# An attention and two-MoE kernel: the first unit's weights P transposed by TensorE instead of by DMA, with work moved between VectorE and ScalarE

## The chip, the cores and the metric

The kernel runs on one core of one Trainium2 chip. The metric is the device time of one execution in microseconds (us). The profile is of one execution, taken by the hardware profiler; the engines in it are PE (TensorE matmul), PEld (TensorE weight load), DVE (VectorE), ACT (ScalarE), POOL (GpSimd) and SP (SyncE, which issues the DMAs here).

## The reference

Three stages, all in float32, on 4 batches of 576 tokens:

```python
scores = scale * q @ k.T                      # 8 heads of 64, causal
bias = -(cum[:, :, :, None] - cum[:, :, None, :])   # cum: running sum of max(s, 0)
attn = softmax(where(causal, -1e9, scores + minimum(bias, 0)))
x = attn @ v                                  # heads joined: (4, 576, 512)
# first MoE
xk = mu_k * x + (1 - mu_k) * x_prev;  xr = mu_r * x + (1 - mu_r) * x_prev
x = sigmoid(xr @ w_r) * (maximum(xk @ w_k, 0) ** 2 @ w_v)
# second MoE
h = maximum(x @ w_in, 0);  u, v = halves of h
v_n = (v - mean) / sqrt(var + 1e-6)
out = (u * (w_spatial @ v_n + b_spatial)) @ w_out
```

The weights arrive as float64 and are turned into float32 on the chip ("decoded", three integer operations of DVE for each block).

## The kernel before, in words

The tokens are cut into nine units of 256. For batch b, A*b* is the first 256 tokens, B*b* the next 256; the last 64 of every batch form the unit T. The order of the attention is ORDER (L48): A0, A1, B0, A2, B1, A3, B2, B3. The first MoE takes the units in the same order, with T before the last of them.

**Attention.** An `Item` (L334) is one head of one unit: kind "G0" is a head of an A unit (two tiles of 128 queries, 128 and 256 keys wide), "G1" a head of a B unit (384 and 512 keys), "T" the tail of a pair of heads (576 columns). `scores` puts the scores in PSUM (tag "s", three banks), `softmax` masks them and takes the row's extreme on DVE (L388) and exponentiates on ACT (L396), and `norm` makes the weights P = e * r, split in two float16 parts: the first part hi by ACT (L429) if the item's kind and batch stand in HI_ACT (L29), else by DVE (L431); the second part lo, the rest, always by DVE (L433). P (three buffers) is then transposed by a DMA issued from SP into eT (L435): for G0 six blocks of 128x128, 192 KB. `pv` (L453) multiplies eT with the parts of v on PE (L479) into one PSUM buffer, and `scaled` brings the result x to SBUF, by ACT (L486) if the kind stands in X_ACT (L31), else by DVE (L488). It comes two items after the pair's last one (PV_LAG). For A0, `first_mix` follows each pair at once: the difference d on POOL (L606, recorded at the helper's line L204), then two operations of DVE that make xm (L608). Four pairs of heads, p = 0 to 3, give the four contraction blocks k = 0 to 3 of the first MoE's matmul.

**First MoE.** For each unit eighteen groups in the order of `seq` (L850): A (L624, `w_k`, eight groups), C (L656, `w_v`, eight, into the PSUM tile cps of tag "c", one buffer) and B (L640, `w_r`, two). ACT evacuates A with a Relu and a Square (L630, L632) from two PSUM buffers.

**Weights.** `w_k` is cut into eight blocks, `w_v` into eight and `w_r` into four; the last two are a list of twelve jobs (L846). A job issues a 512 KB load into one of three buffers (tag "b4"), and `load_double` decodes it on DVE (L509, L512, L514). `weights(n)` (L702) decodes n blocks and keeps three loads ahead. It is called with 8 after A0's attention (the blocks of `w_k`), with W_RATE = 3 before every MoE group (L866), and with 1 after every second attention step past A0 (L788, W_STEP = 2).

**Order.** The attention's steps are laid between the MoE's groups by `target` (L859), which spreads the steps of a unit over a range of groups given by MKS. What stands in the code is not the order on the queues: the program is built with a scheduler that orders each engine's instructions by simulated time (L1137), and each engine then runs its queue in that order.

**Second MoE** (from L881) comes last and is not touched.

Of the kernel before, what the change touches and what calls it, by code (L numbers as in the profile page):

```python
# [7 lines left out]
F32 = mybir.dt.float32  # L8
F32R = mybir.dt.float32r
F16 = mybir.dt.float16  # L10
BF16 = mybir.dt.bfloat16
I32 = mybir.dt.int32
AF = mybir.ActivationFunctionType
# [11 lines left out]
UN = 256  # L25
NU = NTOK // UN
PSC = 32768.0
PV_LAG = 2
HI_ACT = ("G00", "G01", "G10", "T0")  # L29
SQ = "PPPPPDAAD"  # L30
X_ACT = ("2",)  # L31
SQLO = "PPPPPDPPP"
V_STT = (0, 1, 2, 3)
MKS = (10, 9, 0, -2, 2, -2, -2, -2)
W_RATE = 3
W_STEP = 2
W_PRE = 5
W_0 = 2
W_1 = 0
# [8 lines left out]
ORDER = ("A0", "A1", "B0", "A2", "B1", "A3", "B2", "B3")  # L48
# [17 lines left out]
def kernel(  # L66
# [18 lines left out]
    nc = tc.nc  # L85

    def f32(ap):
# [14 lines left out]
    ap_ = at.enter_context(tc.tile_pool(name="att", bufs=1, side="right", reuse_waits="tile"))  # L102
    ps1 = ExitStack()
    pp = ps1.enter_context(tc.tile_pool(name="ps1", bufs=1, space=PSUM, reuse_waits="tile"))
# [10 lines left out]
        out=mask[:, 384:512], in_=mask[:, 384:512], pattern=[[-1, 128]], compare_op=ALU.is_ge,  # L115
        fill=-8.0e9, base=0, channel_multiplier=1)
    nc.gpsimd.memset(maskt, 0.0)
    for g in range(2):
        a = slice(64 * g, 64 * g + 64)
        nc.gpsimd.affine_select(  # L120
            out=maskt[a, 224:288], in_=maskt[a, 224:288], pattern=[[-1, 64]], compare_op=ALU.is_ge,
            fill=-8.0e9, base=0, channel_multiplier=1)

    ident = ap_.tile([128, 128], F32, name="ident")
    nc.gpsimd.memset(ident, 1.0)
    nc.gpsimd.affine_select(
        out=ident, in_=ident, pattern=[[-1, 128]], compare_op=ALU.is_equal, fill=0.0, base=0,
        channel_multiplier=1)

# [74 lines left out]
    def half(g):  # L206
        return slice(64 * g, 64 * g + 64)
# [109 lines left out]
        vparts[b, p] = ((hl[:, 0], hl[:, 1]), PROD3, vm[:, 1:2])  # L317

    eT = {}

    def get_eT(kind, b, p, h=None):
        key = (kind, b, p, h)
        if key not in eT:
            if kind == "1":
                eT[key] = ap_.tile([128, 2, 2, 3, 128], F16, tag="eT1", name="eT1", bufs=T1B)
            elif kind == "2":
                eT[key] = ap_.tile([128, 14, 128], F16, tag="eT2", name="eT2", bufs=T2B)
            else:
                t = ap_.tile([128, 2, 2, 3, 128], F16, tag="eT1", name="eTt", bufs=T1B)
                t = t.rearrange("p a l c i -> p (a l c) i")[:, 0:10]  # L330
                eT[key] = t.rearrange("p (l c) i -> p l c i", l=2)
        return eT[key]

    class Item:  # L334
# [66 lines left out]
        def norm(self):  # L401
            st, e = self.st, self.e
            n = 1 if self.kind == "T" else 2
            nc.vector.tensor_scalar(
                out=st[:, 4:4 + n], in0=st[:, 2:2 + n], scalar1=1e-9, scalar2=1.0 / PSC,
                op0=ALU.add, op1=ALU.mult)
            nc.vector.reciprocal(out=st[:, 6:6 + n], in_=st[:, 4:4 + n])
            P = ap_.tile([128, 1792], F16, tag="P", name="P", bufs=PB)
            if self.kind == "T":
                Pv = P[:, 0:1280].rearrange("p (l c) -> p l c", l=2)  # L410
                nc.gpsimd.memset(Pv[:, :, 576:640], 0.0)
                jobs = [(st[:, 6:7], e[:, 0:576], Pv[:, 0, 0:576], Pv[:, 1, 0:576])]
                dst, nb = get_eT("T", self.b, self.p).rearrange("p l c i -> p (l c) i"), 10
            elif self.kind == "G0":
                Pv = P[:, 0:768].rearrange("p (l c) -> p l c", l=2)
                jobs = [
                    (st[:, 6:7], e[:, 0:128], Pv[:, 0, 0:128], Pv[:, 1, 0:128]),
                    (st[:, 7:8], e[:, 128:384], Pv[:, 0, 128:384], Pv[:, 1, 128:384]),
                ]
                dst = get_eT("1", self.b, self.p)[:, self.h % 2].rearrange("p l c i -> p (l c) i")  # L420
                nb = 6
            else:
                jobs = [
                    (st[:, 6:7], e[:, 0:384], P[:, 0:384], P[:, 384:768]),
                    (st[:, 7:8], e[:, 384:896], P[:, 768:1280], P[:, 1280:1792])]
                dst, nb = get_eT("2", self.b, self.p, self.h), 14
            for r, ein, hi, lo in jobs:
                if self.kind + str(self.b) in HI_ACT:
                    nc.scalar.activation(out=hi, in_=ein, func=AF.Copy, scale=r)  # L429
                else:  # L430
                    nc.vector.tensor_scalar(out=hi, in0=ein, scalar1=r, scalar2=None, op0=ALU.mult)  # L431
            for r, ein, hi, lo in jobs:
                nc.vector.scalar_tensor_tensor(  # L433
                    out=lo, in0=ein, scalar=r, in1=hi, op0=ALU.mult, op1=ALU.subtract)
            nc.sync.dma_start_transpose(out=dst, in_=P[:, 0:128 * nb])  # L435

# [4 lines left out]
    def get_x(key):  # L443
        if key not in xT:
            if key == "T":
                xT[key] = mp.tile([128, NP, B, 65], F32, tag="xt", name="xt")
            else:
                xT[key] = mp.tile([128, NP, UN + 1], F32, tag="x", name="x", bufs=XB)
                if key[0] == "A":
                    nc.gpsimd.memset(xT[key][:, :, 0:1], 0.0)  # L450
        return xT[key]

    def pv(b, p, kind):  # L453
        vt, PROD, esc = vparts[b, p]
        ps = pp.tile([128, 256], F32, tag="pv", name="pvps")
        if kind == "T":
            e = get_eT("T", b, p)
            n = len(PROD)
            for c in range(5):
                for i, (a, l) in enumerate(PROD):  # L460
                    nc.tensor.matmul(  # L461
                        ps[:, 0:128], vt[a][:, c], e[:, l, c],
                        start=(c == 0 and i == 0), stop=(c == 4 and i == n - 1))
        else:
            nch = 2 if kind == "1" else 4
            for c in range(nch):
                for i, (a, l) in enumerate(PROD):
                    for g in range(2):
                        h = 2 * p + g
                        if kind == "1":  # L470
                            e = get_eT("1", b, p)[:, g, l]
                            mv = e[:, 0:2] if c == 0 else e[:, 2:3]
                            t0 = c
                        else:
                            e = get_eT("2", b, p, h)
                            t0 = max(c - 2, 0)
                            o = 3 * l + c
                            mv = e[:, o:o + 7 + l:6 + l] if c < 3 else e[:, 9 + 4 * l:10 + 4 * l]
                        nc.tensor.matmul(  # L479
                            ps[64 * g:64 * g + 64, 128 * t0:256], vt[a][:, c, 64 * g:64 * g + 64], mv,  # L480
                            start=(c == 0 and i == 0), stop=(c == nch - 1 and i == len(PROD) - 1))

        def scaled(out, in_, a=slice(0, 128)):
            by = 1.0 / PSC if esc is None else esc[a]
            if kind in X_ACT:
                nc.scalar.activation(out=out, in_=in_, func=AF.Copy, scale=by)  # L486
            else:
                nc.vector.tensor_scalar(out=out, in0=in_, scalar1=by, scalar2=None, op0=ALU.mult)  # L488

        def evac():  # L490
            done.add((b, p, kind))
            if kind == "T":
                x = get_x("T")
                for g in range(2):
                    a = half(g)
                    scaled(x[a, p, b, 1:65], ps[a, 64 * g:64 * g + 64], a)
            else:
                x = get_x(("A" if kind == "1" else "B") + str(b))
                scaled(x[:, p, 1:UN + 1], ps)
        return evac  # L500
# [55 lines left out]
    def row_blocks(kc, n):  # L556
        return [(slice(k, k + 1), slice(0, n)) for k in range(kc)]
# [144 lines left out]
    def weights(n, ahead=2):  # L702
        for _ in range(n):
            while wjobs and len(wq) <= ahead:
                wq.append(wjobs.pop(0)())
            if wq:
                wq.pop(0)()

    late = []
    ends = {}  # L710
# [71 lines left out]
    pos = [0]  # L782

    def att_to(n):
        while pos[0] < min(n, len(steps)):
            steps[pos[0]]()
            pos[0] += 1
            if pos[0] > ends[ORDER[0]] and pos[0] % W_STEP == 0:  # L788
                weights(1)

    fs = ExitStack()
    fp = fs.enter_context(tc.tile_pool(name="first", bufs=1, side="left", reuse_waits="tile"))
# [50 lines left out]
    wvp = m1.enter_context(tc.tile_pool(name="wv", bufs=1, side="left", reuse_waits="tile"))  # L843
    W["r"], jr = load_weights("wr", wp, w_r, 4, DM, tmp1, col_blocks(4, DM))
    W["v"], jv = load_weights("wv", wvp, w_v, 8, DM, tmp1, row_blocks(8, DM))
    wjobs += jv[0:4] + jr + jv[4:8]  # L846

    groups = []
    for u in range(NU):
# [15 lines left out]
    for gi, (u, kind, m) in enumerate(groups):  # L865
        weights(W_RATE)  # L866
        ev = {"A": moe_A, "B": moe_B, "C": moe_C}[kind](u, m)
# [75 lines left out]
    for i in range(2):  # L943
        a, o = half(i), half(1 - i)
# [197 lines left out]
```

## Time and profile before

| what | us |
|---|---|
| median of three runs | 734.26 (730.25 to 735.81) |
| the profiled execution | 729.34 |
| its span, first to last instruction | 727.6 |
| PE busy in the span | 675.8 (93%) |
| DVE busy | 476.8 (66%) |
| ACT busy | 345.2 (47%) |
| first matmul of the first MoE with the last pair's input (k = 3) begins | 60.49 |

How to read it: the span is what the rows below divide; the 1.7 us between the span and the execution lie around it and are not in any row. A busy share is a mean over stages with different limits, so the rows are taken stage by stage. A bracket such as [1.29 <-DMA eT<-P] gives the idle time of the engine ahead of the instruction and what released it.

### The profile page before, as it was taken

The numbers are of one execution on the slowest core, as the hardware profiler recorded it, in microseconds if no ns is written. First come the engines' busy times: TensorE is split into PE (matmuls) and PEld (weight loads), VectorE is DVE, ScalarE is ACT, GpSimd is POOL, SyncE is SP. The second block draws the span as 40 slices with busy tenths as digits, with TensorE's granted clock in tenths as the row PEclk, the third lists the DMA queues.
The fourth block names the chain that finished last, engine by engine and source line by source line (L and its number), as shares of the span: only waits on it lengthen the run. The fifth ranks groups of instructions, "written<-read, shape, count | busy, mean of one in ns | idle before, by whom it ended". The sixth has DMA issues, their size and how long they took to land.

```text
span 727.6 us, 11854 instructions
## 1 busy us (share of the span) xinstructions
PE 675.8 (93%) x4168; PEld 594.6 (82%) x4168; DVE 476.8 (66%) x1251; ACT 345.2 (47%) x860; POOL 170.7 (23%) x186
## 2 busy tenths in 40 slices
PE   4577999998988999989988999999989999999998
PEld 3455887886877888868877888888888998998998
DVE  7999488778798878998999394030776235035031
ACT  3345359644545676747654423142564343233222
POOL 6114033210432353534432144000540000000000
PEclk9997999999999999999999999999999999999999
DMA  8999368666749787778966731061610110100101
GB/s 231 264 246 222 99 140 185 144 125 139 171 101 179 160 176 190 172 148 202 199 143 124 168 115 59 0 193 50 192 36 16 66 33 1 66 2 1 66 1 66
DMA packets 137027, 88.93 MB, mean 122 GB/s; under 512 B 111396, under 2 KB 120804, under 8 KB 136968
## 3 DMA queue, kind: packets, MB, share of 16 engines
q1 hardware_dynamic: 136968, 88.17, 50.1%
q8 instruction: 33, 0.54, 0.3%
q14 instruction: 26, 0.21, 0.1%
HBM read 52.22 MB, written 9.68 MB: 85 GB/s over the span
## 4 chain that ended last, share of the span: by engine, by line
PE 44%; DVE 7%; issue 2%; DMA 1%; ACT 1%; POOL 0%; SPq 0%; ACTq 0%; DVEq 0%
PE dps L1029 8%; PE dps L1050 7%; PE mmps L624 6%; PE cps L656 6%; PE dps L1009 6%; PE dps L976 6%; PE mmps L640 2%; DVE xm L595 1%; DVE P L433 1%; DVE P L431 1%; DMA wsr<-in_w_spT_dram 1%; PE pvps L479 1%; DVE e L388 1%; PE pvps L461 1%; DVE b L512 1%
## 5 line engine op out<-in xcount | busy, mean ns | idle before, releaser
L624 PE MATMUL mmps<-xm,wk 128*128 128x256 f32 x576 | 143.8, 391 | 5.1 <-ACT e L396 3.0
L656 PE MATMUL cps<-sq,wv 128*128 128x256 f32 x576 | 138.7, 382 | 0.0
L624 PEld LDWEIGHTS mmps<-xm,wk 128*128 128x128 f32 x576 | 109.9, 195 | 22.6 <-ACT e L396 3.2
L656 PEld LDWEIGHTS cps<-sq,wv 128*128 128x128 f32 x576 | 109.1, 191 | 15.0
L396 ACT ACTIVATE e<-e,st 128x128 f32<-128x128 f32 (+3 forms) x128 | 70.8, 554 | 79.3 <-DVE st L388 78.8
L433 DVE SCALAR_TENSOR_TENSOR P<-e,st,P 128x512 f16<-128x512 f32 (+4 forms) x144 | 92.8, 666 | 3.9 <-ACT P L429 3.2
L204 POOL TENSOR_TENSOR kl<-raw,kh 64x576 fp32r<-64x576 f32 (+1 forms) x40 | 55.3, 1382 | 145.6 <-ACT kh L240 124.0
L640 PE MATMUL mmps<-xm,wr 128*128 128x256 f32 x288 | 66.5, 381 | 0.0
L640 PEld LDWEIGHTS mmps<-xm,wr 128*128 128x128 f32 x288 | 54.7, 191 | 7.5
L388 DVE CUSTOM_DVE_ANT_0 e<-sps,mask 128x128 f32<-128x128 f32 (+3 forms) x128 | 57.9, 482 | 1.9 <-PE sps L363 1.1
L630 ACT ACTIVATE kk<-mmps 128x256 f32<-128x256 f32 x72 | 26.8, 374 | 62.4 <-PE mmps L624 62.2
L431 DVE TENSOR_SCALAR P<-e,st 128x128 f16<-128x128 f32 (+3 forms) x92 | 43.4, 509 | 2.2 <-issue 0.4
L363 PE MATMUL sps<-raw 66*128 66x128 f32 (+1 forms) x96 | 28.4, 454 | 13.9 <-DMA raw<-c 10.5
L204 POOL TENSOR_TENSOR qh<-raw,qh 64x320 fp32r<-64x320 f32 (+1 forms) x40 | 40.6, 1015 | 0.2
L665 DVE SCALAR_TENSOR_TENSOR xo<-rg,cps 128x512 f32<-128x512 f32 x18 | 11.6, 679 | 42.6 <-PE cps L656 42.6
L1050 PE MATMUL dps<-gl,woh 128*128 128x288 f32 x128 | 38.2, 298 | 0.0
L1050 PE MATMUL dps<-gh,wol 128*128 128x288 f32 x128 | 38.1, 297 | 0.0
L1050 PE MATMUL dps<-gh,woh 128*128 128x288 f32 x128 | 37.8, 296 | 0.0
L1009 PE MATMUL dps<-x2h,wih 128*128 128x288 f32 x128 | 37.8, 295 | 0.0
L1009 PE MATMUL dps<-x2l,wih 128*128 128x288 f32 x128 | 37.8, 295 | 0.0
L1009 PE MATMUL dps<-x2h,wil 128*128 128x288 f32 x128 | 37.7, 295 | 0.0
L1029 PE MATMUL dps<-wsh,vnh 128*128 128x288 f32 x128 | 37.7, 295 | 0.0
(172 smaller groups left out, 1449.9 us busy)
## 6 DMA issues: line engine op xcount, KB each, us to landing
raw<-in_qkb_dram SPq DMA_DIRECT2D x32, 448.0 KB
vr<-in_v_dram SPq DMA_DIRECT2D x24, 320.0 KB
out_dram<-o SPq DMA_DIRECT2D x32, 144.0 KB
b<-in_w_v_dram SPq DMA_DIRECT2D x8, 512.0 KB
x_d<-xo SPq DMA_DIRECT2D x16, 256.0 KB
b<-in_w_in_dram SPq DMA_DIRECT2D x8, 512.0 KB
raw<-in_qka_dram SPq DMA_DIRECT2D x12, 256.0 KB
b<-x_d SPq DMA_DIRECT2D x8, 288.0 KB
```

The costliest lines, as they stand in the source:

```text
L204: nc.gpsimd.tensor_tensor(out=out, in0=in0, in1=in1, op=ALU.subtract)
L388: nc.vector.tensor_tensor_reduce(out=e[:, off:off + W], in0=self.ps[i], in1=mask[:, 512 - W:512], scale=-0.125, scalar=3.0e38, op0=ALU.add ...
L396: nc.scalar.activation(out=e[:, off:off + W], in_=e[:, off:off + W], func=AF.Exp, scale=-1.0, bias=st[:, i:i + 1], accum_out=st[:, 2 + i:3 ...
L431: nc.vector.tensor_scalar(out=hi, in0=ein, scalar1=r, scalar2=None, op0=ALU.mult)
L433: nc.vector.scalar_tensor_tensor(out=lo, in0=ein, scalar=r, in1=hi, op0=ALU.mult, op1=ALU.subtract)
L624: nc.tensor.matmul(ps[:, 0:UN], W["k"][:, k, 128 * m:128 * m + 128], mix[u, "k"][:, k], start=(k == 0), stop=(k == 3))
L640: nc.tensor.matmul(o, W["r"][:, k, 128 * m:128 * m + 128], mix[u, "r"][:, k], start=(k == 0), stop=(k == 3))
L656: nc.tensor.matmul(cps[u][:, m], W["v"][:, k, 128 * m:128 * m + 128], sq[u, k], start=(k == 0 and m % 2 == 0), stop=(k == 7 and m % 2 == 1))
L976: nc.tensor.matmul(ps, a[:, k, j:j + 128], w[:, k, 512:1024], start=(n == 0), stop=(n == 11))
L1009: nc.tensor.matmul(ps[:, 0:HB], w[:, k, 128 * m:128 * m + 128], a[:, k, HB * hf:HB * hf + HB], start=(n == 0), stop=(n == 11))
L1029: nc.tensor.matmul(ps[:, 0:HB], vn, ws, start=(n == 0), stop=(n == len(pairs) - 1))
L1050: nc.tensor.matmul(ps[:, 0:HB], w[:, k, 128 * m:128 * m + 128], a[:, k], start=(n == 0), stop=(n == 11))
```

## The change

The list of jobs changes in one line: five blocks of `w_v` stand ahead of those of `w_r` instead of four. The call of `weights` in `att_to` goes, and W_RATE falls from 3 to 1. HI_ACT gains the A units of batches 2 and 3 and the B unit of batch 1. X_ACT keeps all B units ("2") and gains the A units of batches 0 and 1 ("10", "11"). A0's eight items are transposed by six PE instructions each into a PSUM tile of tag "c" (the tag of cps), half a tile for each head of a pair, and one ACT copy brings each head's result to eT.

```diff
-HI_ACT = ("G00", "G01", "G10", "T0")
+HI_ACT = ("G00", "G01", "G02", "G03", "G10", "G11", "T0")
-X_ACT = ("2",)
+X_ACT = ("20", "21", "22", "23", "10", "11")
-W_RATE = 3
-W_STEP = 2
+W_RATE = 1
...
+    idh = ap_.tile([128, 128], F16, name="idh")
+    nc.gpsimd.tensor_copy(idh, ident)
...
+    turned = {}
...
-            nc.sync.dma_start_transpose(out=dst, in_=P[:, 0:128 * nb])
+            if self.kind == "G0" and self.b == 0:
+                self.transpose(P, dst, nb)
+            else:
+                nc.sync.dma_start_transpose(out=dst, in_=P[:, 0:128 * nb])
+
+        def transpose(self, P, dst, nb):
+            if self.h % 2 == 0:
+                turned[self.p] = pp.tile([128, 4, UN], F32, tag="c", name="tps")
+            ps = turned[self.p].bitcast(F16).rearrange("p (g a) n -> p g (a n)", g=2)[:, self.h % 2]
+            for i in range(nb):
+                j = slice(128 * i, 128 * i + 128)
+                nc.tensor.transpose(ps[:, j], P[:, j], idh)
+            nc.scalar.activation(
+                out=dst.rearrange("p l i -> p (l i)"), in_=ps[:, 0:128 * nb], func=AF.Copy)
...
-            if kind in X_ACT:
+            if kind + str(b) in X_ACT:
...
-            if pos[0] > ends[ORDER[0]] and pos[0] % W_STEP == 0:
-                weights(1)
...
-    wjobs += jv[0:4] + jr + jv[4:8]
+    wjobs += jv[0:5] + jr + jv[5:8]
```

## Rows read from the trace of the kernel before

**Rows 1.** Windows by stage: PE, PEld, DVE, ACT, POOL busy, clock, DMA share, GB/s.

```profile
20.00:42.00 22.00, 14.68 (x80) 10.87 (x82) 21.63 (x68) 8.40 (x30) 2.99 (x5) 1.00 0.94 248
42.00:48.00 6.00, 4.20 (x19) 3.44 (x16) 5.40 (x20) 2.77 (x10) 1.31 (x3) 1.00 1.04 226
48.00:60.50 12.50, 6.22 (x51) 4.15 (x50) 12.50 (x40) 6.79 (x22) 5.24 (x6) 0.83 0.97 254
60.50:67.00 6.50, 6.26 (x17) 4.06 (x19) 6.50 (x17) 5.07 (x16) 4.58 (x4) 0.53 0.75 205
67.00:107.00 40.00, 40.00 (x246) 34.35 (x243) 27.22 (x69) 18.08 (x43) 8.45 (x9) 1.00 0.62 139
107.00:450.00 343.00, 324.60 (x2045) 276.96 (x2044) 290.81 (x809) 197.54 (x503) 115.74 (x117) 0.99 0.69 154
450.00:727.60 277.60, 270.49 (x1695) 253.31 (x1693) 96.97 (x189) 99.12 (x216) 19.83 (x14) 0.99 0.17 52
```

**Rows 2.** Timeline of PE: start, us, line, operation, count, idle before and releaser.

```profile
23.24 0.37 PE L479 MATMUL pvps<-eT,vr 128*64 128x256 f16 x1 [1.29 <-DMA eT<-P]
...
48.77 1.36 PE L479 MATMUL pvps<-eT,vr 128*64 128x256 f16 x20
...
50.18 0.92 PE L363 MATMUL sps<-raw 66*128 66x128 f32 x4
...
60.49 2.07 PE L624 MATMUL mmps<-xm,wk 128*128 128x256 f32 x4 [0.48 <-DVE xm L608]
...
63.15 3.68 PE L624 MATMUL mmps<-xm,wk 128*128 128x256 f32 x8 [0.24 <-ACT kk L630]
...
67.48 1.99 PE L624 MATMUL mmps<-xm,wk 128*128 128x256 f32 x8
...
104.62 1.00 PE L461 MATMUL pvps<-eTt,vhl 128*128 128x128 f16 x15
```

**Rows 3.** Timeline of DVE in the first unit.

```profile
16.36 0.75 DVE L433 SCALAR_TENSOR_TENSOR P<-e,st,P 128x256 f16<-128x256 f32 x1
...
41.43 0.47 DVE L433 SCALAR_TENSOR_TENSOR P<-e,st,P 128x256 f16<-128x256 f32 x1
...
53.83 0.41 DVE L488 TENSOR_SCALAR x<-pvps 128x256 f32<-128x256 f32 x1
...
59.98 0.46 DVE L608 SCALAR_TENSOR_TENSOR xm<-d,muk,x 128x256 f32<-128x256 f32 x1
```

**Rows 4.** Timeline of POOL: the last pair's d, with what runs ahead.

```profile
55.70 1.31 POOL L204 TENSOR_TENSOR qh<-raw,qh 64x320 fp32r<-64x320 f32 x1
57.09 0.68 POOL L204 TENSOR_TENSOR d<-x 128x256 f32<-128x256 f32 x1
```

**Rows 5.** Windows of DVE's decoding alone: wv in the first two, wr in the third.

```profile
30.00:42.00 12.00, 3.93 (x7) 1.00 0.79 184
42.00:60.40 18.40, 3.13 (x5) 0.89 0.98 245
...
42.00:60.40 18.40, 5.93 (x9) 0.89 0.98 245
```

**Rows 6.** Groups of instructions by line: count, busy us, mean ns.

```profile
L431 DVE TENSOR_SCALAR P<-e,st 128x128 f16<-128x128 f32 (+3 forms) x92 | 43.4, 509 | 2.2 <-issue 0.4
L630 ACT ACTIVATE kk<-mmps 128x256 f32<-128x256 f32 x72 | 26.8, 374 | 62.4 <-PE mmps L624 62.2
L429 ACT ACTIVATE P<-e,st 128x128 f16<-128x128 f32 (+4 forms) x52 | 25.3, 534 | 10.5 <-DVE st L407 8.9 <-ACT e L396 1.5
L647 ACT ACTIVATE rg<-mmps 128x512 f32<-128x512 f32 x18 | 10.2, 585 | 16.3 <-PE mmps L640 16.3
```

**Rows 7.** Waits of PE: us in total, times, longest.

```profile
PE mmps L624 <- ACT e L396: 3.0, 1, 3.0
...
PE sps L349 <- ACT x L486: 2.4, 1, 2.4
```

## The prediction

> **What bounds the kernel now.** I read the windows by stage first [rows 1], because PE's 93% is a mean. From 67 to 107 us PE is busy for 40.00 of 40.00 us; from 107 to 450 it lacks 18.4 us (343.0 - 324.6); behind 450 it lacks 7.1 in a stage that the change leaves alone. The holes are in front: 7.3 us from 20 to 42, 1.8 from 42 to 48, 6.3 from 48 to 60.5, together 15.4. In the same stretches DVE is full: 21.63 of 22.0, 5.40 of 6.0, 12.50 of 12.5, 6.50 of 6.5. So up to 67 us the first unit, A0, is made by a saturated DVE while PE waits for it, and afterwards PE sets the pace, with DVE at 85% (290.8 of 343) close behind.
>
> Second I read the timelines of PE, DVE and POOL along A0's end. The last P of A0 is finished at 41.90 (41.43 + 0.47) [rows 3]. The products of the last pair begin at 48.77 and end at 50.13 [rows 2]. DVE takes the result x at 53.83, 3.7 us later [rows 3]; POOL forms d at 57.09, 2.9 us after x was there, straight behind the qh part of a split of heads for a later unit [rows 4]; DVE makes xm at 59.98, 2.2 us after d ended at 57.77 [rows 3]; PE begins the fourth contraction block at 60.49 [rows 2], and the first MoE can run. From the last P to that matmul 18.6 us pass, of which the work itself is about 4.
>
> Third, what stood in front of A0 on DVE: decoding of wv took 3.93 us between 30 and 42, and wv and wr together 9.06 (3.13 + 5.93) from 42 to 60.4 [rows 5]. That work is not needed before the first MoE runs.
>
> Fourth, PE's clock. [...] The twelve matmuls at 60.49 and 63.15 took 5.75 us; the eight at 67.48 took 1.99, which for twelve is 3.0 [rows 2]. The low clock costs 2.8 us.
>
> **The change part by part.**
>
> *Transposes on PE.* The trace has no such transpose. Before, the first head's P ended at 17.11 (16.36 + 0.75) [rows 3], and PE, idle, was released by its eT at 23.24 [rows 2]: 6.1 us. After, six matmuls with 128 columns of float16: fifteen of that shape took 1.00 us at the full clock, 67 ns each [rows 2], so 0.4 us, or 0.8 at half; then a copy of 128x768 out of PSUM. ACT's 128x256 takes 0.374 and its 128x512 0.585 [rows 6], so a further 256 columns give 0.80. [...] The 48 transposes are 3.2 to 6.4 us of new PE work. They lie before the first MoE, in the 9.1 us of holes from 20 to 48; if these are gone they cost their full length. The eight copies (6.4 us) go into ACT's 16.8 idle us from 20 to 48 (28.0 - 8.40 - 2.77) [rows 1]. SP loses eight issues; nothing is moved past them. What is queued behind a transpose on PE, which now waits for P, is the scores of A1's heads, and only DVE, which is full, would use these.
>
> [...]
>
> *A0's tail.* With the decoding out of the way the last P is done between 38.0 (41.9 - 3.9) and 41.9. Then 1.8 to eT, 1.4 for the products, 0.4 for x, now on ACT, where nothing like DVE's queue stands in front (a Copy of 128x256 takes 0.374), 0.7 for d, 2.2 until xm as before, 0.9 for its two operations: 7.4 together. The first MoE's k = 3 begins at 45.4 to 49.3. If POOL again has the split ahead (2.9) and x waits 3.7 as it did, the latest is 55.9. I take 48.0, inside the two nearer ends, as the POOL wait may recur in part: 12.5 us earlier.
>
> *What PE gets of it.* Two pieces of PE work that stood between 48 and 60.5 belong to A1 and now come behind the start: a set of scores (0.92 at 50.18) and the products of one pair (1.36, as at 48.77) [rows 2], 2.3 us; leaves 10.2. The ledger of holes gives the same from the other side: the stretch from 20 to 48 would hold its old work of 18.9 us, 4.8 of transposes (the middle) and what A0 had later, the 1.4 of products and a contraction block of 1.0 (half of the 1.99 at 67.48), 26.1 of 28; holes fall from 15.4 to 1.9, and 4.8 of work is added: 8.7. I take 9.5. Of the 2.8 us of low clock I count half, 1.4: PE has fewer holes, but its first matmuls may again be slow (0 to 2.8).
>
> *Later decoding.* Nothing is removed: DVE still decodes twelve blocks, some 13 us of it now behind 48. Its cover is DVE's idle time in 67 to 107, 12.8 us, and the 3.3 us (8 x 0.41) of x's that ACT takes. From 20 to 107 DVE does 73.2 us; less 3.3 this has to fit into about 77, 91%. If PE's holes at 91% were double those of 107 to 450 (5.4% at 85%), the 45 us of the first unit would lose 4.8; at none, 0. I count nothing and keep 4.8 for the range. The loads of these jobs go out on SP one by one between groups instead of three at once; each still leads its decode by two jobs, about two groups.
>
> *Hi parts and x to ACT.* 24 heads have two hi parts each, 48 operations. At the mean of 0.509 DVE loses 24 us and at 0.534 ACT gains 26 [rows 6] (means over mixed shapes). In 107 to 450 DVE falls from 291 to 267 and ACT rises from 198 to 223 of 343 [rows 1]. The longest waits of PE there are on ACT, 3.0 and 2.4 us [rows 7], so easing DVE takes at most part of the 18.4 us, and loading ACT may add to it. I take a gain of 1.0, between a gain of 7 (what is not such a wait, 13.0, halved) and a loss that the third rival prices.
>
> **Sum.** 9.5 + 1.4 + 1.0 = 11.9. The profiled execution took 729.3, so 717.4; the median shown is 734.3, 5.0 above it, so 722.4, and I say 722. One per cent, 7.3 us, is about what a measurement of this kernel tells from no change; the three runs lie 5.6 apart.
>
> **The rivals.**
>
> 1. *DVE alone held A0, the DMA was hidden.* For it: DVE is full from 20 to 67, so an earlier eT may only wait longer in DVE's queue; PE was busy for 4.2 of 6.0 us before the last products. Against: the 6.1 us with PE idle at 23.24. Then only the decoding (3.9) and the wait of x (3.3 of 3.7) go: 7.2 earlier, less 2.3 for A1 and about 1.5 for transposes with nothing to hide in: 3.4, so 731. [...]
>
> 2. *The decoding does not move.* The order on the queues is the scheduler's, and wv was decoded at 30 us, before its place in the code; smaller calls of `weights` may leave it there. Then P ends at 41.9, POOL's 2.9 stays, and k = 3 begins at 52.2: 8.3, less 1.5 for A1, plus 0.5 of clock: 7.3, so 727.
>
> 3. *ACT becomes the bound, slower.* Place: the A units of batches 2 and 3 and the B unit of batch 1, 24 heads. ACT runs in order, and it must empty one of two PSUM buffers of the A groups within a group; a pair of hi parts (2 x 0.534) put ahead of an evacuation that PE already waits for, as in the 3.0 us wait [rows 7], holds PE. At 0.9 us for each head that is 21.6 us against 11: 745. It decides against the change from 0.46 us a head. Against it: ACT is at 58% in that stage and would be at 65%.
>
> **How the numbers follow.** Forecast 0.65: its own range is 717 (all 2.8 of clock, 3 more in the middle, holes closed) to 728 (start at 49.3 and 4.8 lost to DVE); nearly all of it is faster by over 1% (under 726.9). Rival 1: 0.13, all but 0.02 within 1%. Rival 2: 0.10, on the edge, half each way. Rival 3: 0.12, two thirds over 741.6, the rest within 1%, since it may be partial. Faster 0.61 + 0.02 + 0.05 = 0.68; slower 0.08; within 1% the rest, 0.24. For eight in ten I go from 711, if the tail starts at 45.4 and DVE's relief gives 7, to 737, part of rival 3.
>
> **What would show it.** Right: the k = 3 matmul near 48; x of A0 on ACT within a microsecond of its products; wv and wr decoded mostly behind it; PE's holes in 20 to 60.5 under 6 us; no stretch at 0.53 clock behind it, or a shorter one; the group of twelve blocks done before the C groups ask. Wrong: k = 3 behind 53; wv still decoded near 30; C groups waiting for DVE's wv; in 100 to 440 more than 18 us of holes, released by ACT. If k = 3 comes at 48 and the time stays, the gain was given back there, and the windows by stage will say where.

## The result, and the profile after

The median after is 722.12 us (718.41 to 723.99, four runs) beside 734.6 before in the same rounds; the ratio is 0.986, interval [0.9816, 0.9904]. The forecast of 722 holds and so does its sign; its reasons, as the runs below show, mostly do not. The profiled execution after is the slowest of its four (723.99, span 722.2) and that of before was the fastest of its runs, so the two spans lie only 5.4 us apart.

The windows by stage of the kernel after, with the cuts of [rows 1] (PE, PEld, DVE, ACT, POOL busy, clock, DMA share, GB/s):

```profile
20.00:42.00 22.00, 18.80 (x109) 13.45 (x111) 22.00 (x66) 12.33 (x36) 5.54 (x6) 0.96 0.50 178
42.00:48.00 6.00, 4.67 (x42) 3.56 (x40) 6.00 (x20) 4.64 (x14) 0.62 (x1) 0.78 0.75 231
48.00:60.50 12.50, 10.42 (x55) 8.35 (x52) 12.45 (x43) 8.69 (x28) 2.88 (x4) 0.90 0.98 237
60.50:67.00 6.50, 6.50 (x46) 5.47 (x44) 5.00 (x17) 4.16 (x15) 1.06 (x2) 1.00 0.94 277
67.00:107.00 40.00, 37.10 (x222) 30.67 (x221) 29.21 (x73) 21.58 (x54) 15.75 (x16) 0.96 0.57 146
107.00:450.00 343.00, 328.51 (x2054) 279.54 (x2053) 271.20 (x752) 214.06 (x545) 112.65 (x110) 0.99 0.67 152
```

Subtract PE's busy time from each stretch: the holes from 20 to 60.5 fall from 15.4 to 6.6 us, those from 107 to 450 from 18.4 to 14.5, and 2.9 us of new ones stand in 67 to 107, where there were none. DVE is as full as before up to 60.5. Behind 107 it fell by 19.6 us and ACT rose by 16.5.

PE's timeline in A0 (start, us, operation, count, idle before and its releaser):

```profile
22.55 0.85 PE L450 MATMUL tps<-idh,P 128*128 128x128 f16 x6
...
46.06 0.28 PE L450 MATMUL tps<-idh,P 128*128 128x128 f16 x2 [0.34 <-DVE P L437]
47.34 1.76 PE L496 MATMUL pvps<-eT,vr 128*64 128x256 f16 x19 [0.99 <-ACT eT L451]
...
49.02 1.82 PE L641 MATMUL mmps<-xm,wk 128*128 128x256 f32 x4
...
52.98 1.03 PE L641 MATMUL mmps<-xm,wk 128*128 128x256 f32 x4
```

The fourth contraction block starts at 52.98, 7.5 us before the 60.49 of [rows 2], not at 48. DVE's timeline in the same unit shows why not 48:

```profile
31.65 0.83 DVE L526 TENSOR_SCALAR wv<-b 128x512 int32<-128x512 int32 x1
...
45.17 0.83 DVE L437 SCALAR_TENSOR_TENSOR P<-e,st,P 128x256 f16<-128x256 f32 x1
...
52.18 0.47 DVE L625 SCALAR_TENSOR_TENSOR xm<-d,muk,x 128x256 f32<-128x256 f32 x1
```

A0's last P ends at 46.0, 4.1 us later than the 41.90 of [rows 3]; what came forward lies behind it. `wv` is still decoded from 31.65 on. Windows of that decoding alone, the kernel after (DVE busy is the third figure behind the length):

```profile
30.00:42.00 12.00, 0.00 (x0) 0.00 (x0) 4.01 (x6) 0.93 0.33 107
42.00:53.00 11.00, 0.00 (x0) 0.00 (x0) 5.55 (x10) 0.77 0.71 216
```

Before it was 3.93 in the first of these stretches [rows 5]: the decoding did not leave. With 0.67 us for `wr`, 10.2 us of decoding stand ahead of the fourth block, 13.0 before.

POOL's timeline, the last pair's d:

```profile
49.75 0.99 POOL L207 TENSOR_TENSOR d<-x 128x256 f32<-128x256 f32 x1 [4.03 <-ACT x L503]
```

The products of the last pair end at 49.10 (47.34 + 1.76), and d begins 0.65 us later, with x on ACT between; before it was 7.0 us (50.13 to 57.09), with DVE's queue and POOL's split of heads ahead [rows 2 to 4]. From the end of the last P to the products it is 1.3 us (46.0 to 47.34) where it was 6.9 (41.90 to 48.77). So the start of k = 3 comes from two waits, 5.5 us at the transpose and 6.3 between products and d, less the 4.1 us by which P is later.

Groups of the kernel after by line (count, busy us, mean ns, idle before):

```profile
L450 PE MATMUL tps<-idh,P 128*128 128x128 f16 x48 | 7.1, 290 | 2.6 <-ACT eT L451 1.9 <-DVE P L437 0.7
L451 ACT ACTIVATE eT<-tps 128x768 f16<-128x768 f16 x8 | 6.4, 797 | 1.6 <-PE tps L450 1.6
L433 ACT ACTIVATE P<-e,st 128x128 f16<-128x128 f32 (+3 forms) x100 | 47.9, 525 | 15.1 <-DVE st L411 7.0 <-DVE st L408 5.4 <-ACT e L400 1.5
L435 DVE TENSOR_SCALAR P<-e,st 128x384 f16<-128x384 f32 (+2 forms) x44 | 24.7, 590 | 0.9
```

The 48 transposes took 7.1 us of PE, beyond the upper end of 6.4; the copies took what was estimated (0.797 each). The hi parts moved as expected: 92 to 44 on DVE, 52 to 100 on ACT [rows 6].

PE's waits in the kernel after (us in total, times, longest):

```profile
PE pvps L478 <- DMA eTt<-P: 5.6, 4, 2.8
PE mmps L641 <- ACT e L400: 3.3, 1, 3.3
```

The first is new as a large item: the products of the tails T wait for their DMA transposes.

How much of the earlier start reaches the next unit is read from DVE's timelines at the second unit, A1: its first xm, in the kernel before and in the kernel after:

```profile
101.13 3.54 DVE L595 SCALAR_TENSOR_TENSOR xm<-dx,muk,x 128x256 f32<-128x256 f32 x4 [0.48 <-POOL dx L204]
```

```profile
100.00 3.72 DVE L612 SCALAR_TENSOR_TENSOR xm<-dx,muk,x 128x256 f32<-128x256 f32 x4
```

It begins 1.1 us earlier, so of the 7.5 us by which A0's first MoE starts earlier the second unit sees little. In the two kernels below that have the transposes and not the moves to ACT it begins at 99.8 and 96.6: there more of the lead arrives, and the time is still longer than before.

### The profile page after: what moved, and what is told of

It is laid out like the page before. It is cut to its first block, busy times and chain, and to the rows that moved or that the text cites. A ratio compares the mean times of both kernels' runs of the same rounds, so it can differ in the third digit from the quotient of the medians.

```text
span 722.2 us, 11976 instructions
## 1 busy us (share of the span) xinstructions
PE 680.6 (94%) x4216; PEld 597.5 (83%) x4216; DVE 457.9 (63%) x1195; ACT 371.4 (51%) x924; POOL 173.2 (24%) x187
## 5 line engine op out<-in xcount | busy, mean ns | idle before, releaser
L673 PE MATMUL cps<-sq,wv 128*128 128x256 f32 x576 | 140.7, 384 | 0.0
L673 PEld LDWEIGHTS cps<-sq,wv 128*128 128x128 f32 x576 | 108.9, 192 | 15.4
L437 DVE SCALAR_TENSOR_TENSOR P<-e,st,P 128x512 f16<-128x512 f32 (+4 forms) x144 | 89.1, 636 | 10.1 <-ACT P L433 9.3
L433 ACT ACTIVATE P<-e,st 128x128 f16<-128x128 f32 (+3 forms) x100 | 47.9, 525 | 15.1 <-DVE st L411 7.0
L1044 PE MATMUL dps<-wsl,vnh 128*128 128x288 f32 x128 | 37.7, 294 | 0.0
L1044 PE MATMUL dps<-wsh,vnl 128*128 128x288 f32 x128 | 37.7, 294 | 0.0
```

What stands on the lines that cost most here:

```text
L437: nc.vector.scalar_tensor_tensor(out=lo, in0=ein, scalar=r, in1=hi, op0=ALU.mult, op1=ALU.subtract)
L673: nc.tensor.matmul(cps[u][:, m], W["v"][:, k, 128 * m:128 * m + 128], sq[u, k], start=(k == 0 and m % 2 == 0), stop=(k == 7 and m % 2 == 1))
L1044: nc.tensor.matmul(ps[:, 0:HB], vn, ws, start=(n == 0), stop=(n == len(pairs) - 1))
```

## The experiments

Each kernel is the one after with parts undone, unless a diff says more. Ratios are to the kernel before, run beside them, whose medians were 732.61 (the first four), 732.46 (the next four) and 732.21 (the last four).

**All combinations of the three parts.** The parts are the transposes, the later decoding, and the moves to ACT (hi parts and x).

The transposes alone:

```diff
-HI_ACT = ("G00", "G01", "G02", "G03", "G10", "G11", "T0")
-X_ACT = ("20", "21", "22", "23", "10", "11")
-W_RATE = 1
+HI_ACT = ("G00", "G01", "G10", "T0")
+X_ACT = ("20", "21", "22", "23")
+W_RATE = 3
+W_STEP = 2
...
+            if pos[0] > ends[ORDER[0]] and pos[0] % W_STEP == 0:
+                weights(1)
...
-    wjobs += jv[0:5] + jr + jv[5:8]
+    wjobs += jv[0:4] + jr + jv[4:8]
```

> The kernel before with only the transposes of A0 on PE. Theory 1 (the transposes and x on ACT bring the first MoE's start forward, the moves to ACT close holes behind 107 us, the later decoding is worth nothing because DVE still decodes wv among A0's heads): k = 3 begins at 54 to 56 instead of 60.5, time 728 to 730, ratio 0.991 to 0.995. Theory 2 (the later calls of the decoding are the main gain): k = 3 at 58 or later, ratio 0.996 to 1.000. Theory 3 (DVE alone held A0, the DMA transposes were hidden): no change of the start, ratio 1.000 to 1.004 for the added PE work.

The decoding edits alone (lists as before, and the transposes off):

```diff
-            if self.kind == "G0" and self.b == 0:
+            if False:
                 self.transpose(P, dst, nb)
```

> The kernel before with only the decoding edits (one block for each group, none between attention steps, five wv blocks first). Theory 1: wv still decoded from near 31 us, k = 3 within 2 us of 60.5, ratio 0.997 to 1.003. Theory 2: k = 3 at 54 to 56, ratio 0.990 to 0.994.

The moves to ACT alone (transposes off, decoding undone):

> The kernel before with only HI_ACT and X_ACT changed. Theory 1: k = 3 some 2 to 4 us earlier because x of A0 no longer waits in DVE's queue, PE's holes in 107 to 450 down by about 4 of 18.4, ratio 0.990 to 0.994. Theory 2: only the holes behind 107, ratio 0.994 to 0.997. If ACT were near its bound (the slower rival of the prediction): ratio over 1.0.

The change without the decoding edits:

> The changed kernel with the decoding edits undone. Theory 1: as the changed kernel, ratio 0.984 to 0.988, k = 3 within 2 us of 53. Theory 2: half the gain lost, ratio 0.992 or more, k = 3 behind 56.

The change without the transposes:

> The changed kernel with A0 transposed by DMA again; the moves to ACT and the later decoding stay. Theory A (what counts is the work taken off DVE; the first MoE's start is worth nothing): as the moves alone, ratio 0.978 to 0.984. Theory B (each edit reorders all queues, and half a per cent either way is that order's luck): more than half a per cent away from the 0.981 of the moves alone. The prediction's sum would want 0.994 to 0.998, since it gave the moves 1.0 us.

The change without the moves to ACT:

> The changed kernel with HI_ACT and X_ACT as before: transposes and later decoding alone. Theory A: as the transposes alone, ratio 1.002 to 1.008, although k = 3 begins at 53 to 56. Theory B: further than 0.5% from that. The prediction's sum: 0.985 to 0.988.

| transposes | decoding | moves to ACT | ratio | interval | k = 3 begins | after the first matmul |
|---|---|---|---|---|---|---|
| yes | | | 1.0055 | 1.0029 to 1.0081 | 54.84 | 42.4 |
| | yes | | 0.999 | 0.9967 to 1.0014 | 60.71 | 50.4 |
| | | yes | 0.9811 | 0.9781 to 0.9841 | 57.54 | 46.2 |
| yes | | yes | 0.9892 | 0.9867 to 0.9917 | 52.2 | 41.9 |
| | yes | yes | 0.9806 | 0.9762 to 0.985 | 57.29 | 47.1 |
| yes | yes | | 1.0056 | 1.002 to 1.0092 | 52.97 | 42.7 |
| yes | yes | yes | 0.986 | 0.9816 to 0.9904 | 52.98 | 41.8 |

The last column is there because the profiles do not begin their work at the same time: PE's first matmul, released by a load, starts between 10.2 and 13.5 us. Before, it starts at 10.49, and k = 3 follows 50.0 us later. The first matmul of the kernel before, and of the one in which it is latest (the idle transposes, below):

```profile
10.49 9.32 PE L363 MATMUL sps<-raw 66*128 66x128 f32 x28 [10.49 <-DMA raw<-c]
```

```profile
13.54 6.77 PE L369 MATMUL sps<-raw 66*128 66x128 f32 x20 [13.54 <-DMA raw<-c]
```

Three of these kernels missed every theory written down for them. The transposes alone brought the start forward as Theory 1 said, but the time lies above even Theory 3's 1.004. The moves alone gained more than any range named (0.990 was the lowest). Without the decoding edits k = 3 comes as Theory 1 said, and the ratio lies between the two ranges.

Four pairs of rows differ in one part each (the kernel before is the row of 1). The transposes cost 0.55, 0.81, 0.66 and 0.54%, on average 0.64% or 4.7 us. The decoding edits give between -0.32 and +0.01%, on average 0.8 us less. The moves to ACT give -1.89, -1.63, -1.84 and -1.96%, on average 13.4 us less. The parts add up, and the order by time is not the order by the start of k = 3: with the transposes alone it starts 5.7 us earlier (7.6 counted from the first matmul) and the kernel is slower.

Where that start went is read from the windows of two kernels, first the one before, over the whole of A0's stretch:

```profile
20.00:60.50 40.50, 25.09 (x145) 18.46 (x145) 39.53 (x126) 17.96 (x62) 9.54 (x12) 0.95 0.97 246
```

and the one with the transposes alone:

```profile
20.00:60.50 40.50, 33.28 (x203) 24.71 (x202) 40.50 (x129) 25.34 (x74) 9.88 (x12) 0.97 0.66 215
...
107.00:450.00 343.00, 320.20 (x2003) 272.19 (x2002) 297.77 (x806) 195.34 (x497) 118.32 (x118) 0.97 0.67 154
```

PE's holes from 20 to 60.5 fall from 15.4 to 7.2 us, and those from 107 to 450 rise from 18.4 to 22.8; the other stretches have 2.9 more, 1.8 of them ahead of 20 us, where the first matmul is 2.0 us later. Over the span the idle time of PE is 51.0 us (736.1 - 685.1), 51.8 before. So most of the holes that close in front open again elsewhere, and 48 transposes (6.9 us busy) came on top. DVE is busy for all of A0's stretch, before and now. That an earlier eT gains nothing because DVE is full fits this, but no run shows it by itself. The two profiled executions lie 8.5 us apart and the medians 3.5, so such a ledger is good to some 5 us.

The moves to ACT alone, the same windows:

```profile
20.00:60.50 40.50, 26.41 (x158) 18.96 (x156) 39.67 (x125) 19.59 (x67) 10.20 (x12) 0.87 0.93 235
...
107.00:450.00 343.00, 331.48 (x2067) 282.03 (x2066) 269.01 (x746) 215.30 (x548) 118.68 (x118) 0.99 0.65 151
```

Here the holes in front hardly shrink (14.1); those behind 107 do, to 11.5, and the idle time of the whole span is 44.5 us (717.2 - 672.7).

**The two moves apart.** The hi parts alone (X_ACT as before):

> The kernel before with HI_ACT alone changed: 48 hi parts from DVE to ACT, some 21 us of DVE behind 107 us; nothing in A0. Theory A: nearly the whole gain, ratio 0.981 to 0.986, k = 3 within 2 us of 60.5. Theory C (x of A0 and A1 on ACT is what brings the gain): 0.992 to 0.998.

x alone (HI_ACT as before):

> The kernel before with X_ACT alone changed: eight x of A0 and A1 from DVE to ACT, 3.3 us of DVE. Theory A: k = 3 some 3 us earlier, and no gain from it, ratio 0.996 to 1.001. Theory C: 0.985 to 0.990.

Hi parts 0.9955 [0.9926, 0.9985]; x 0.9899 [0.9857, 0.9942]. The smaller move has the larger effect, by intervals that just overlap: eight operations of DVE, 3.3 us together (8 x 0.413), are worth some 7 us (4 to 10 by the interval). The start does not explain it: with x alone k = 3 begins at 61.94, 1.4 us later than before and not 3 earlier as Theory A said, and with the hi parts alone at 61.41. From 20 to 60.5 DVE is busy for 37.3 of 40.5 us with x alone, 39.5 before; the work taken off became idle time there, most of it one wait of 3.2 us for a load of weights. (The profiled execution took 727.44 us; the median is 724.72.) Together the two give 1.89%, against 1.46 if they added up; the intervals allow either.

**Load or wait?** x on ACT does two things: DVE has less to do, and x does not wait in DVE's queue. The first of these is put back, to the moves to ACT alone: DVE makes each x of A0 and A1 once more into a tile that nobody reads.

```diff
+    spare = ap_.tile([128, UN], F32, name="spare")
...
                 nc.scalar.activation(out=out, in_=in_, func=AF.Copy, scale=by)
+                if kind == "1":
+                    nc.vector.tensor_scalar(
+                        out=spare, in0=out, scalar1=1.0, scalar2=None, op0=ALU.mult)
```

> The moves to ACT alone, and in addition DVE copies each x of A0 and A1 (128x256, eight copies of about 0.4 us) into a spare tile that nobody reads; x itself still comes from ACT at once. Theory D (load: DVE never idles from 20 to 67 us, so each us put there shifts the attention): the share of x is lost again, ratio 0.987 to 0.993 against 0.981 without the copies. Theory E (wait: what helped is that x no longer stands in DVE's queue and PE's product buffer comes free): 0.978 to 0.984.

It measured 0.9919 [0.9891, 0.9948] where the moves alone have 0.9811. Its group, and its window behind 107:

```profile
L507 DVE TENSOR_SCALAR spare<-x 128x256 f32<-128x256 f32 x8 | 4.6, 569 | 0.3 <-ACT x L505 0.3
```

```profile
107.00:450.00 343.00, 326.87 (x2056) 279.75 (x2055) 279.05 (x761) 217.91 (x552) 114.45 (x118) 0.99 0.67 154
```

Eight operations put back on DVE cost 1.1%, 7.9 us, which is x's share or a little more, although x itself stayed on ACT. So Theory E fails: that x no longer waits in DVE's queue is not what brought the gain. Theory D's ratio is met, but its reason, a DVE that never idles, is not shown. The copies alone, in two windows of DVE:

```profile
20.00:67.00 47.00, 1.72 (x4) 0.85 0.97 238
67.00:107.00 40.00, 2.83 (x4) 1.00 0.61 152
```

Only four of them, 1.72 us, lie where DVE is nearly full (45.5 of 47 us). The other four lie behind 67, where it is busy for 27.2 of 40 us, and most of the loss appears by the end of that stretch. The first xm of A1, with the moves alone and with the copies:

```profile
96.01 3.53 DVE L613 SCALAR_TENSOR_TENSOR xm<-dx,muk,x 128x256 f32<-128x256 f32 x4 [0.20 <-POOL dx L208]
```

```profile
102.77 2.26 DVE L617 SCALAR_TENSOR_TENSOR xm<-dx,muk,x 128x256 f32<-128x256 f32 x4
```

That is 6.8 us later, or 6.0 counted from the first matmul (11.37 and 12.15); k = 3 was later by 1.8 and 1.0 (59.31 against 57.54). PE's clock differs too. From 60.5 to 67, with the moves alone and with the copies (the figure behind the five engines is the granted clock):

```profile
60.50:67.00 6.50, 5.47 (x41) 4.37 (x40) 6.13 (x21) 4.78 (x16) 1.52 (x2) 1.00 0.96 259
```

```profile
60.50:67.00 6.50, 6.50 (x34) 4.62 (x33) 6.39 (x18) 6.23 (x18) 2.94 (x2) 0.64 0.84 195
```

Load on DVE, the order that the scheduler makes with eight more operations, and the low clock behind it are not separated. The holes behind 107 are 16.1 us again.

The same for the hi parts: DVE makes the 48 moved ones once more.

```diff
+    spare = ap_.tile([128, 512], F16, name="spare")
...
                     nc.scalar.activation(out=hi, in_=ein, func=AF.Copy, scale=r)
+                    if self.kind + str(self.b) in ("G02", "G03", "G11"):
+                        nc.vector.tensor_scalar(
+                            out=spare[:, 0:hi.shape[-1]], in0=ein, scalar1=r, scalar2=None, op0=ALU.mult)
```

> The moves to ACT alone, and in addition DVE makes the 48 hi parts of the A units of batches 2 and 3 and of the B unit of batch 1 a second time into a spare tile, some 21 us of DVE; P still takes ACT's. Theory D (DVE's load sets the pace of the attention): ratio 0.986 to 0.991. Theory E for these (the order hi by ACT, lo by DVE is what helps, DVE has room): 0.979 to 0.984.

0.984 [0.9807, 0.9873]. Its group and window:

```profile
L437 DVE TENSOR_SCALAR spare<-e,st 128x128 f16<-128x128 f32 (+3 forms) x48 | 18.9, 393 | 0.8
```

```profile
107.00:450.00 343.00, 326.36 (x2060) 278.38 (x2059) 287.18 (x798) 216.33 (x550) 116.78 (x118) 1.00 0.66 153
```

DVE has nearly the load of before behind 107 (287 of 343), and only 0.3% comes back, which this measurement cannot tell from nothing. The ratio is the upper end of Theory E's range. The holes behind 107 are 16.6 us here (343.0 - 326.4), as many as with x's copies, so the holes of one profile do not tell the two apart; PE's busy time over the span is 668.3 us, 672.7 with the moves alone. What the ratios show is that 18.9 us of DVE work behind 107 cost less than 4.6 us in the first two units.

**Is it the earlier start or the transposes themselves?** The moves to ACT alone, and A0's P both transposed by PE into a tile that nobody reads and turned by the DMA as before:

```diff
+    spare = ap_.tile([128, 6, 128], F16, name="spare")
...
             if self.kind == "G0" and self.b == 0:
-                self.transpose(P, dst, nb)
-            else:
-                nc.sync.dma_start_transpose(out=dst, in_=P[:, 0:128 * nb])
+                self.transpose(P, spare, nb)
+            nc.sync.dma_start_transpose(out=dst, in_=P[:, 0:128 * nb])
```

> The moves to ACT alone, and in addition TensorE transposes A0's P and ACT copies the result into a spare tile that nobody reads; eT still comes by DMA. Theory F (the transposes cost their own PE time, 7 us, and the earlier start is given back): ratio 0.987 to 0.992. Theory G (they cost nothing by themselves; the later P and the holes come from putting them on the path): 0.979 to 0.984.

0.9872 [0.9833, 0.9911], where the same kernel with transposes that are used has 0.9892 and the one with none 0.9811. Its group of transposes, and PE's timeline at k = 3:

```profile
L451 PE MATMUL tps<-idh,P 128*128 128x128 f16 x48 | 6.9, 292 | 4.1 <-ACT spare L452 4.1
```

```profile
60.63 2.08 PE L642 MATMUL mmps<-xm,wk 128*128 128x256 f32 x4 [1.96 <-DVE xm L626]
```

The same step with transposes that are used (the change without the decoding edits):

```profile
52.20 1.03 PE L642 MATMUL mmps<-xm,wk 128*128 128x256 f32 x4
```

Transposes whose result nobody waits for cost as much as those that bring k = 3 forward from 60.6 to 52.2 us (from 47.1 to 41.9 counted from the first matmul). So the cost goes with their work, on PE and in ACT's copies, which this run does not separate; what the earlier start gives is not to be seen.

**Does ACT become the bound?** The change without the transposes, and with it all remaining hi parts of the B units and all x of the A units on ACT:

```diff
-HI_ACT = ("G00", "G01", "G02", "G03", "G10", "G11", "T0")
-X_ACT = ("20", "21", "22", "23", "10", "11")
+HI_ACT = ("G00", "G01", "G02", "G03", "G10", "G11", "G12", "G13", "T0")
+X_ACT = ("20", "21", "22", "23", "10", "11", "12", "13")
```

> The changed kernel without its transposes, with all hi parts of A and B units and all x on ACT, another 17 us off DVE and 22 us onto ACT. Theory D: faster still, ratio 0.972 to 0.978 against 0.981. If ACT becomes the bound, the slower rival of the prediction: over 0.985, with PE's waits on ACT longer than 10 us in 107 to 450.

0.9781 [0.9744, 0.9817], 716.67 us. Its window behind 107:

```profile
107.00:450.00 343.00, 331.25 (x2076) 282.59 (x2075) 252.71 (x705) 234.71 (x587) 116.05 (x118) 0.99 0.66 151
```

ACT at 235 of 343 does not hold PE: the holes there are 11.8 us, beside 11.5 with ACT at 215. It is the fastest of all, though not to be told from the change without the transposes (717.38), and Theory D's 0.972 to 0.978 is missed: another 17.5 us off DVE behind 107 (252.7, 270.2 without) gave nothing that can be told from noise. Both beat the kernel after.

## Why the prediction was right and wrong

The number came out because two errors of opposite sign met, which is luck.

| term of the sum | predicted, us | measured, us |
|---|---|---|
| transposes, A0's tail and clock | -9.5 - 1.4 | +4.7 |
| later decoding | 0 | -0.8 |
| hi parts and x to ACT | -1.0 | -13.4 |
| sum | -11.9 | -9.5 |

The measured terms are the means over four pairs at a kernel before of 732.5 us; the whole change measures -1.4%, or -10.3, in its own rounds. The tail's term also drew on the decoding and on x, so its row compares the step as the prediction argued it with the part that was to carry it.

*"Hi parts and x to ACT … I take a gain of 1.0."* This is the step that was mis-sized, and it holds the whole gain. I looked for PE waits that name DVE behind 107 and found little [rows 7]. x's 3.3 us were entered as the cover for decoding and as 3.3 us off one wait, and are worth some 7. The put-back run shows that this comes with eight operations fewer on DVE and not with the wait; by what way they cost more than twice their time stays open, since half of them lie where DVE idles. The hi parts, made behind 107, helped by a way that stays open too. The upper end kept for this term was 7; the measured 13.4 lies outside it.

*"A0's tail … I take 9.5."* The start came forward, if by 7.5 us instead of 12.5, and was worth nothing. The ledger counted PE's holes from 20 to 60.5 as time, supposing that PE, once started, has work. It has not: 2.9 us of new holes stand in 67 to 107, and A1's first xm begins only 1.1 us earlier. The sign given for this case held in part: k = 3 came early, if not at 48, and most of the lead was gone by the second unit. The argument against the first rival, PE idle for a transpose at 23.24 [rows 2], showed a wait that is real in A0, and closing it was worth no time.

*"The last P is done between 38.0 and 41.9."* It ends at 46.0. In the four kernels with used transposes it ends at 44.2 to 46.0, in the moves to ACT alone at 42.1. What else DVE puts ahead of it there follows from the scheduler's order, which I did not separate.

*"Then 1.8 to eT."* No run shows the 0.2 us in it that stands on top of 0.8 for the transposes and 0.80 for the copy. In the kernel after the last P ends at 46.0, its copy to eT runs from 46.49 to 47.29 and the products begin at 47.34: 1.3 us. ACT's timeline there:

```profile
46.49 0.80 ACT L451 ACTIVATE eT<-tps 128x768 f16<-128x768 f16 x1
```

*"Of the 2.8 us of low clock I count half."* The stretch from 60.5 to 67 is at full clock now (1.00, 0.53 before), but 42 to 48 fell from 1.00 to 0.78 and 67 to 107 from 1.00 to 0.96: the low clock has moved more than it has gone. That fewer holes of PE raise the clock is not shown: from 42 to 48 PE was busy for 4.67 us at 0.78, and before for 4.20 at 1.00 [rows 1].

*Transposes "lie in the holes".* They took 7.1 us, not 4.8. They did lie in the holes, and the kernels with them are 4.7 us slower all the same, two thirds of their length.

*"Later decoding … I count nothing."* Right in the sum (0.1%, not to be told from zero), wrong in "with the decoding out of the way": it stayed at 31 us, as the first half of the second rival says. What left the front is most of `wr`, 5.93 us before and 0.67 after.

*Rivals.* The first (DVE alone held A0, the DMA was hidden) had the transposes' sign, a cost that finds nothing to hide in, if 1.5 us for the 4.7 measured; it was wrong that the start would not move with them: the time did not fall (1.0055 with the transposes alone), but A0 did wait for the DMA, whose eT came 6.1 us after P for the first head [rows 2 and 3], for k = 3 came 5.7 us earlier without it. It had no price for the moves to ACT either. The second was right on where decoding stays. The third is refuted: ACT took still more hi parts and nothing was lost.

*Open.* What gives x and the hi parts their shares, the latter since DVE's load behind 107 put back takes at most a part of it; the queue order that the scheduler makes with them is a candidate that no run separates, though one part's effect stays within 0.4% whatever the other parts are. PE's mean granted clock is another: 0.984 over the four runs with the moves alone, 0.978 over the 19 before beside them. Why the new holes behind 60.5 fall where they do, wait by wait. And whether transposes would pay with A0's DVE work halved was not tried.

## What to carry to other kernels

Do not count the idle time of an engine as a gain before you know what it will do with it: with the transposes alone, 8.2 us of PE's holes closed in front and the kernel became slower. Look at the next unit's first step, and see whether the lead arrives there. Do not price an operation by its own time: eight short ones put back on DVE in the first two units cost more than 48 put back later with four times the work, and the busy share of the stretch did not say which. A total that agrees says nothing of its terms; one part alone and all but one part do.

## What the runs showed of the hardware that was not expected

What a PE operation took in A0 depended on when it ran more than expected: four equal matmuls took 1.82 us at 49.02 and 1.03 at 52.98 in the kernel after, where the granted clock was 0.64 from 49 to 51 and 1.00 from 51 to 54. Six transposes took 0.85 us at 22.55 there and 0.50 at 48.38 in the kernel with the transposes alone. The granted clock was 1.00 from 22 to 24 for the first, and for the second 1.00 from 42 to 48 and 0.91 from 48 to 60.5, so that the clock of these stretches does not explain this pair (PE timeline of the latter):

```profile
48.38 0.50 PE L451 MATMUL tps<-idh,P 128*128 128x128 f16 x6
```

So the 48 came to 148 ns each (7.1 / 48), more than twice the 67 ns of products with the same shape [rows 2]. The DMA transpose of 192 KB that was read took 6.1 us from P to eT [rows 2 and 3], and replacing eight of them brought no time. ACT's copy of 128x768 out of PSUM took 0.797 us on average; the slope between its 256- and 512-column operations (0.374 and 0.585 us [rows 6]) gives 0.80.
